# Attention beside a gated feed-forward on one core: the first head group's queries of blocks 1 to 3 spread by DMA, landing times in the plan, and four more planner figures in the table

## The chip, the cores and the metric

The kernel runs on one core of a Trainium2 chip. The metric is device time in microseconds for one execution, as a median over several runs. The profiled execution is a run of its own, with its own time; its span goes from its first to its last instruction.

## The reference

The inputs are bfloat16, with 2048 rows of 512 features. The output mixes an attention block and a feed-forward block on the same x, row by row, with a gate.

```python
g = sigmoid((x * gate_w).sum(-1, keepdims=True))
# A: attention, 32 heads of 16
q, k, v = split(x @ wqkv)                        # [32 heads, 2048, 16] each
p = softmax(q @ k.T * 16 ** -0.5)                # 2048 x 2048 per head
a = concat_heads(p @ v) @ wo
# B: feed-forward of width 1792, on x as well
b = (silu(x @ w_gate) * (x @ w_up)) @ w_down
out = g * a + (1 - g) * b
```

The greatest part of the work is the exponential: 32 heads x 2048 x 2048 values.

## The kernel before

**Tiles and units.** The 32 heads form 8 groups (G) of four. The 2048 queries form 4 blocks (QB) of 512. A group with a block is a *unit*; there are 32. The list UNIT takes group 0 of all four blocks first (units 0 to 3), and then, block by block, groups 1 to 7. Each unit has 16 (KT) *key tiles* of 128 keys, so there are 512 tiles, also called *slots* where they count time. The scores of one tile fill four PSUM banks, one for each head: 128 keys (partitions) by 512 queries.

**Two ways to the exponential.** ScalarE takes most tiles: one activation reads two or three banks and writes them to the buffer e_all (22 places of one bank). VectorE takes the others. It evicts the scores from PSUM as scaled 16-bit integers, whose bits read as bfloat16 are a rough exponential; then it makes shifted or masked copies, so that the sum of two or of four products with the values comes close to the true exponential. `groups[n]` is 2 or 4: with 2, two masked copies and a multiplication; with 4, three shifted copies, of which GpSimd makes one (`lifted`) while VectorE reads PSUM. GpSimd may also take a multiplication or a second copy (`take_over`). The integer tiles lie in tiles named c_t, or in kaug or wd_t where these have room. TensorE multiplies each copy with the values (vaug) into an output bank of the unit. These products are drained in the order of the units (`pv_list`, from the unit `closed` on). At most EB pairs of exponentials may wait in e_all before a product is forced.

**Queries.** The queries of two heads that are neighbours in a row group must not meet, so each group's queries are held twice (index v): in version v the rows of the heads with j % 2 != v are zero. For groups 1 to 7 (`q_pieces`, line 673) the queries are evicted from PSUM to the tile qst, and DMAs on the SyncE queue put each head's rows in place; VectorE and GpSimd work out a bound from them in the tile aq, whose rows follow by DMA as well. For group 0 (`q0_pieces`, line 705) the projection has padded columns; after the bound is added in PSUM, `variants` (line 733) copies the bank to qst and multiplies it on VectorE by the two columns of a mask, vsel, into the two versions. Those of blocks 0 and 1 lie in qx, those of blocks 2 and 3 in the tile on.

**The planner.** The order of all instructions on each engine is fixed while the program is built. A planner keeps a model time for each engine (`plan.pe`, `plan.dve`, `plan.act`, `plan.pool`) and a time for each PSUM bank, and takes one step after another in the loop from line 2061: scores for ScalarE, with scores of a VectorE tile alongside where `wants` asks for them (`choose`, line 877, and `emit_group`, line 985), products with values, or a piece of the other work (projections, the feed-forward, the normalising). The other work is in chains with a slot at which they are released, a deadline, and chains that they come after. A chain of queries keeps `done_at`, the slot, and `t_done`, the model time at which it was finished. `q_of[u]` is the chain that brings unit u's queries.

`v_unit` (line 2015) says from which unit VectorE may take its next tile, always the last tile that is left of that unit. Its rules, before:

```python
if y_live[0] >= NY or home_at(max(vu, au) * KT) >= 1e9 or sum(v[0] for v in vops) > 4.9 or (au, at_) < (0, 2):
    return None
while vu < UNITS:
    if vu > au + 1 or vu in q_of and not (q_of[vu].done() and (vu < QB or plan.slot >= q_of[vu].done_at + 3)):
        return None
    ...
        if plan.dve + busy + (LEAD if vu < UNITS - 1 else LAST) <= end:
            return vu
    vu += 1
```

Here `au` is the unit that ScalarE is in, `vops` are the copies and multiplications queued for VectorE, and `end` is the model time at which ScalarE would be through the tiles of the unit that are left.

**The table.** About 27 figures weigh the planner's choices: what a step is worth (W3, W4, N1, N2, NEXT ...), when side work may go (HUNGRY, KEEP, FIRST ...), limits (EB, NY), whether GpSimd takes over (TAKE_C, TAKE_P, GLEAD, WINDOW). The table WEIGHTS (line 160) holds rows of them under slot numbers, and `begin` (line 1917) puts a row in force when its slot begins.

In the profile each operation stands at the line of the helper that records it: L260 is every matmul, L263 every activation, L276 every operation of VectorE and GpSimd and every DMA of the SyncE queue in the main part.

Of the kernel before, what the change touches and what calls it, by code (L numbers as in the profile page):

```python
# [18 lines left out]
class Chain:  # L19
# [3 lines left out]
    def __init__(self, pieces, release, deadline, after=(), gap=0, cond=None, begun=()):  # L23
        self.begun = list(begun)
        self.pieces = list(pieces)
        self.i = 0
        self.owed = 0
        self.release = release
        self.deadline = deadline
        self.after = list(after)  # L30
        self.gap = gap
        self.cond = cond
        self.done_at = None
        self.t_done = 0.0

# [46 lines left out]
def kernel(  # L82
# [13 lines left out]
    P = 128  # L96
# [21 lines left out]
    EB = 10  # L118
    NE = 22
    NP = 8  # L120
    NY = 3
# [12 lines left out]
    HUNGRY = 0.351  # L134
    KEEP = 2
    FED = 5.562
    W3 = -0.276
    N1 = 6.533
    N2 = 2.473
# [15 lines left out]
    SPARE = 0.665  # L155
# [241 lines left out]
    class Plan:  # L397
        pe = dve = act = pool = 0.0
        mode = last = None
        seq = 0  # L400
        slot = -1
        chain = None

    plan = Plan()
    owed = []
    asides = []
    work_at = []
    banks = [0.0] * NP
    held = [None] * NP

    FLIP, UNIT_US, PIECE_US, COLS_US, TURN = 0.1055, 0.2157, 0.0024, 0.2133, 0.0105
    TO_ACT, ACT_FIX, ACT_COL, ACT_IN = 0.485, 0.064, 0.4265, 0.167
    ACT_PE, DVE_PE, PE_DVE, ACT_DVE = 0.055, 0.08, 0.24, 0.06
    GPS = 1
    OWN = 0
    POOL_IN, POOL_FIX, POOL_ONE, POOL_PE, POOL_OVER = 0.12, 0.12, 0.43, 0.2, 0.1
    TAKE_P = 1
    FACE = 1
    TAKE_C = 1
    GLEAD = 5.764  # L420
    WINDOW = 1.503

# [24 lines left out]
    def pay(i=0):  # L447
        ready, cost, f, c, key, fast = owed.pop(i)
        spend_v(cost, ready, key, fast)
        keep, plan.chain = plan.chain, None  # L450
        f()
        if fast:
            fast_last[0] = last_of[vec.engine.engine]
        plan.chain = keep
        if c is not None:
            c.owed -= 1
            if c.done():
                c.done_at = plan.slot
                c.t_done = plan.dve + DVE_PE
# [245 lines left out]
    def q0_pieces(qb):  # L705

        st = {}

        def landed(p):
            st["p"] = p  # L710
            later(0.6, mag, key=("aq", qb))
            later(0.21, clear, key=("aq", qb), fast=True)

        def mag():
            vec.tensor_copy(out=mt[:, 5, :], in_=st["p"][:, :])

        def clear():
            vec.tensor_scalar(out=mt[:, 5, :].bitcast(U16), in0=mt[:, 5, :].bitcast(U16), scalar1=0x7FFF, scalar2=None,
                              op0=ALU.bitwise_and)

        def bound():
            bound_add(st["p"], kneg0, mt[:, 5, :])
            spend("C", 1)
            variants(st["p"], q0[qb], work.tile([P, QBW], BF16, tag="qst", name="qst")[:, :])
        return (columns(DC, "qp", lambda dc: wpad[0][:, dc, :], lambda dc: xT[:, dc, qb * QBW:(qb + 1) * QBW], landed),
                [(1, bound, False)])

    def bound_add(p, kn, aq):
        for j in range(4):
            mm(p[32 * j:32 * j + 32, :], lhsT=kn[:, 32 * j:32 * j + 32], rhs=aq, start=False, stop=True,  # L730
               tile_position=(0, 32 * j), skip_group_check=True)

    def variants(p, to, q, more=()):

        def copy():
            vec.tensor_copy(out=q, in_=p[:, :])
            m_free(p, plan.dve)

        def select():
            for v in range(2):  # L740
                vec.tensor_scalar(out=to[:, v, :], in0=q, scalar1=vsel[:, v:v + 1], scalar2=None, op0=ALU.mult)
        key = object()
        later(0.6, copy, key=key)
        later(0.4, select, key=key, fast=True)
        for cost, f in more:
            later(cost, f, key=key)
# [238 lines left out]
    def emit_group(parts_, ds, rel):  # L985
        nonlocal quarter, at_, begun
        s = [i for p in parts_ for i in p]
        w = len(s)
        bs = next_banks(w)
        begun = 1  # L990
        start = max(plan.pe + (FLIP if plan.mode != "R" else 0.0), rel,
                    *(q_of[b // 4 // KT].t_done for b in bs if b // 4 // KT in q_of))
        spare[0] = min(spare[0] + max(0.0, horizon() - LATEST - start - 0.1), 1.5)
        plan.pe = start
        plan.mode = "R"
        for i in s:
            banks[i] = None
        for i in ds:
            banks[i] = None
        fit = fitting(w)  # L1000
        extra = len(ds) > len(fit)
        riders = (d_slots() if extra else fit)[:len(ds)]
        for k, b in enumerate(bs):
            score(psum[:, s[k], :], b, 32 if riders or w != 2 else 64)
        done = 0
        todo = []
        for p in parts_:
            e0 = e_run(len(p))
            e_next[0] = e0 + len(p)
            for k, b in enumerate(bs[done:done + len(p)]):  # L1010
                e_of[b] = e_all[:, e0 + k, :]
                e_slot[b] = e0 + k
            todo.append((p, bs[done:done + len(p)], e0))
            done += len(p)
        if riders:
            emit_d(riders, ds)
        spend("R", 2 if extra else 1)
        flush_act()
        ready = start + TO_ACT

        for p, pb, e0 in todo:
            def exp(p=p, pb=pb, e0=e0, w=len(p)):
                act(out=e_all[:, e0:e0 + w, :], in_=psum[:, p[0]:p[0] + w, :], func=ACT.Exp, scale=inv_sqrt_dh)
                plan.act = max(plan.act + ACT_FIX, ready + ACT_IN) + ACT_COL * w
                for i in p:
                    banks[i] = plan.act + ACT_PE
                for b in pb:
                    e_end[b] = plan.act + ACT_PE
            exps.append((ready, exp, len(p)))
        for _ in bs:  # L1030
            quarter += 1
            if quarter == 4:
                quarter = 0
                at_ += 1
                begun = 0
                forward()
                begun = int(quarter > 0)
            else:
                begun = 1
        begun = int(quarter > 0)  # L1040
# [193 lines left out]
    def aside_now():  # L1234
        job = asides[0]
        _, f, width, k, done, c = job
        ins = f(slice(k, k + min(width, QBW // 2)))
        if fast_last[0] is not None:
            tc.add_manual_dep(ins.ins, fast_last[0].name,
                              mybir.DependencyInfo(mybir.DependencyClass.Sync, mybir.DependencyReason.DATA), reason="beside reads of PSUM")  # L1240
        plan.pool = max(plan.pool, plan.dve + POOL_IN) + POOL_FIX + 0.48
        job[3] = k + QBW // 2
        if job[3] < width:
            return
        asides.pop(0)
        if c is not None:
            c.owed -= 1
        if done is not None:
            done()
        if c is not None and c.done():  # L1250
            c.done_at = plan.slot
            c.t_done = plan.pool + POOL_PE
# [417 lines left out]
    for g in (3, 4):  # L1670
        ones_rows(vec, g)
    for g in range(5, G):
        ones_rows(gps, g)
# [77 lines left out]
    for qb in range(1, QB):  # L1751
        d = qb * KT
        q, bd = q0_pieces(qb)
        q = pace.add(q, 0, d - 13, [known])
        bd = pace.add(bd, 0, d - 11, [q])
        need.setdefault(d - 5, []).append(bd)
        q_of[qb] = bd
    for qb in range(QB):
        for b in range(NB):
            d = UNIT.index((qb, max(2 * b, 1))) * KT  # L1760
            after = []
            if qb == 0:
                ks = []
                for tb in range(QB):
                    prev = [pace.add(k_pieces(b, tb), 3, d - 40 + tb, prev)]
                    ks += prev

                def bnd(b=b):
                    later(2.46, lambda: k_bound(b), fast=True)
                after = prev = [pace.add([(0.2, bnd, False)], 0, d - 34, ks)]  # L1770
# [3 lines left out]
            elif b == 1:  # L1774
                rel = UNIT.index((qb - 1, 6)) * KT + 1 if qb else 0
            else:
                rel = UNIT.index((qb, 2 * b - 2)) * KT + 1 if (qb, b) != (0, 2) else UNIT.index((0, 2)) * KT + 1
            q = pace.add(q_pieces(qb, b), rel, d - QLEAD, after)
            need.setdefault(d - 12, []).append(q)
            for g in {max(2 * b, 1), 2 * b + 1}:  # L1780
                q_of[UNIT.index((qb, g))] = q
# [427 lines left out]
```

## Time and profile before

| what | value |
|---|---|
| median of 3 runs | 749.18 us (749.06 to 749.56) |
| the profiled execution | 749.8 us, span 748.0 us |
| granted TensorE clock | 1.00 |
| first exponential starts | 13.26 us |
| exponentials on ScalarE | 751 instructions, 708.7 us busy |
| first evictions of VectorE's tiles | 525 instructions in c_t, kaug, wd_t |
| GpSimd busy | 276.4 us (37%) |

A share of busy time is an average over stages. Busy times of a group of instructions are unions, so that the busy time over the count is the pitch of one, which can be less than the mean duration of one where two overlap.

### The profile page before, as it was taken

To read this page: it belongs to the slowest core of one execution; us is meant where nothing else is said; L and a number is where in the kernel's file an instruction comes from. 1 tells how busy PE (TensorE), PEld (TensorE's weight loads), DVE (VectorE), ACT (ScalarE), POOL (GpSimd) and SP (SyncE) were. 2 spreads that over 40 slices of the span, in tenths; PEclk is the share of its full clock that TensorE was granted. 3 is DMA by queue.
4 is the path that set the end of the run, shared out by engine and by line. 5 is a ranking of instruction groups with operands and counts; after the bars stand their busy time and mean duration, and the time that the engine had idled before them with its cause. 6 is when DMAs were issued, how large, how long until landed. Compare 5 with 4: busy or idle time off the path is not lost.

```text
span 748.0 us, 23841 instructions
## 1 busy us (share of the span) xinstructions
PE 728.8 (97%) x10047; PEld 236.8 (32%) x10047; DVE 717.1 (96%) x1172; ACT 733.0 (98%) x823; POOL 276.4 (37%) x398
## 2 busy tenths in 40 slices
PE   8999999999999999999999999999999999999997
PEld 4323333333333333333333333333233323332332
DVE  7889999999999999999999999999999999999995
ACT  5999999999999999999999999999999999999996
POOL 5234023433454342444433423444444335343200
PEclk9999999999999999999999999999999999999999
DMA  9002012243120003221100041202001322100010
GB/s 217 18 2 58 9 33 56 59 122 87 41 56 13 13 21 92 59 55 39 36 16 22 19 104 46 66 21 59 18 13 27 76 68 58 32 20 13 15 37 30
DMA packets 91027, 34.51 MB, mean 46 GB/s; under 512 B 75488, under 2 KB 90472, under 8 KB 90920
## 3 DMA queue, kind: packets, MB, share of 16 engines
q1 hardware_dynamic: 89192, 32.66, 18.4%
q8 instruction: 79, 1.29, 0.7%
q10 hardware_dynamic: 1728, 0.33, 0.2%
q14 instruction: 28, 0.23, 0.1%
HBM read 21.55 MB, written 2.35 MB: 32 GB/s over the span
## 4 chain that ended last, share of the span: by engine, by line
ACT 60%; PE 23%; DVE 12%; issue 3%; DMA 1%; SPq 0%; DVEq 0%
ACT e_all L263 57%; PE psum L260 23%; DVE c_t L276 8%; ACT th L263 3%; DVE mt L276 1%; DVE kaug L276 1%; DVE gs L276 1%; DMA on<-osb 1%; DVE osb L276 0%; DVE kpart L276 0%; DVE qst L276 0%; SPq L276 0%; ACT xT L263 0%; DVE rd L276 0%; DVE o_t L276 0%
## 5 line engine op out<-in xcount | busy, mean ns | idle before, releaser
L263 ACT ACTIVATE e_all<-psum 128x1024 bf16<-128x1024 f32 (+1 forms) x751 | 708.7, 1113 | 1.4 <-PE psum L260 1.2
L276 DVE TENSOR_SCALAR c_t<-psum 128x512 uint16<-128x512 f32 x441 | 293.7, 689 | 8.1 <-PE psum L260 6.2
L260 PE MATMUL psum<-qx,kaug 32*128 32x512 bf16 (+1 forms) x1632 | 246.2, 385 | 7.2 <-ACT e_all L263 6.6
L276 POOL TENSOR_TENSOR c_t<-c_t,lift 128x256 int32<-128x256 int32 (+1 forms) x175 | 120.9, 700 | 177.1 <-DVE c_t L276 126.1
L260 PE MATMUL psum<-e_all,vaug 128*32 128x512 bf16 (+3 forms) x1980 | 168.2, 335 | 0.8 <-ACT e_all L263 0.4
L260 PEld LDWEIGHTS <-kaug 32*128 32x128 bf16 (+1 forms) x2048 | 74.1, 91 | 264.0 <-ACT e_all L263 188.3
L260 PEld LDWEIGHTS <-vaug 128*32 128x32 bf16 x3992 | 97.1, 95 | 130.7 <-issue 93.5
L260 PE MATMUL psum<-c_t,vaug 128*32 128x512 bf16 (+3 forms) x1720 | 134.4, 338 | 0.8 <-DVE c_t L276 0.4
L276 DVE TENSOR_SCALAR c_t<-c_t 128x2048 uint16<-128x2048 uint16 x181 | 125.4, 701 | 1.4 <-PE psum L260 0.7
L276 POOL TENSOR_TENSOR c_t<-c_t 128x256 bf16<-128x256 bf16 (+2 forms) x65 | 54.7, 858 | 98.0 <-DVE c_t L276 79.1
L260 PE MATMUL psum<-xT,wg 128*32 128x512 bf16 x896 | 73.5, 383 | 0.2 <-DVE c_t L276 0.2
L260 PE MATMUL psum<-wd_t,mt 128*32 128x512 bf16 x896 | 72.9, 382 | 0.0
L260 PE MATMUL psum<-xT,wu 128*32 128x512 bf16 x896 | 70.8, 383 | 0.9 <-DVE gs L276 0.8
L276 DVE TENSOR_SCALAR kaug<-psum 128x512 uint16<-128x512 f32 x76 | 51.1, 685 | 1.3 <-PE psum L260 0.8
L260 PE MATMUL psum<-q,kaug 32*128 32x512 bf16 (+1 forms) x256 | 49.8, 385 | 0.5 <-ACT e_all L263 0.4
L276 DVE TENSOR_TENSOR c_t<-c_t 128x2048 bf16<-128x2048 bf16 (+1 forms) x36 | 43.9, 1219 | 0.0
L260 PE MATMUL psum<-xT,wqk 128*32 128x512 bf16 x512 | 41.0, 383 | 0.2 <-DVE osb L276 0.2
L276 DVE SCALAR_TENSOR_TENSOR gs<-th,psum 128x512 bf16<-128x512 bf16 x56 | 38.1, 680 | 1.0 <-ACT th L263 0.9
L276 DVE SCALAR_TENSOR_TENSOR mt<-gs,psum 128x512 bf16<-128x512 bf16 x56 | 38.0, 679 | 0.5 <-PE psum L260 0.4
L263 ACT ACTIVATE th<-psum 128x512 bf16<-128x512 f32 x56 | 38.5, 687 | 0.0
L276 POOL TENSOR_TENSOR aq<-aq,kb 128x256 bf16<-128x256 bf16 x32 | 19.3, 612 | 40.7 <-DVE c_t L276 38.6
L260 PEld LDWEIGHTS <-mt 128*32 128x32 bf16 (+1 forms) x1045 | 24.3, 95 | 29.3 <-issue 21.3
(129 smaller groups left out, 474.0 us busy)
## 6 DMA issues: line engine op xcount, KB each, us to landing
wg<-in_B_w_gate_dram SPq DMA_DIRECT2D x56, 128.0 KB
wu<-in_B_w_up_dram SPq DMA_DIRECT2D x56, 128.0 KB
on<-osb SPq DMA_DIRECT2D x120, 16.0 KB
rb<-rr SPq DMA_DIRECT2D x15, 128.0 KB
wd_t<-in_B_w_down_dram SPq DMA_DIRECT2D x7, 256.0 KB
qx<-qst SPq DMA_DIRECT2D x96, 16.0 KB
qx<-aq SPq DMA_DIRECT2D x96, 16.0 KB
out_dram<-o_t SPq DMA_DIRECT2D x12, 128.0 KB
```

The lines of the kernel that those rows point to most:

```text
L260: return ordered(nc.tensor.matmul(out, lhsT=lhsT, rhs=rhs, **kw), [lhsT, rhs], [out])
L263: ordered(nc.scalar.activation(out=out, in_=in_, **kw), [in_, *kw.values()], [out])
L276: return ordered(f(*a, **kw), reads, [out])
```

## The change

Four things change.

1. The queries of group 0, blocks 1 to 3: the bank is still copied to qst by VectorE, but the two multiplications by the mask are gone. A new function, `apart`, issues four DMAs on the SyncE queue, each of which puts one head's 32 rows in the version where it belongs. The other version's zeros come from two GpSimd memsets at the start, put before three memsets of kaug that were there. Block 0 still uses `variants`.
2. The planner knows when queries land: each chain has a `lag`, 2.3 us for chains of queries, which is added to `t_done`. `v_unit` now asks for `t_done <= plan.pe`, in place of three slots after `done_at`; `emit_group` also waits for the queries of the unit whose VectorE tile goes alongside.
3. The projections of keys for the other groups wait until the model time of TensorE is 6.9 us (LANDED).
4. Four figures that were constants become part of each row of the table, whose rows are new but for one (slot 344): SLACK (0.04 before: how far a step may overrun a gap), LEAD (8.0 before), LINE (1.3 before: the VectorE evictions in line beyond which `wants` asks for none) and STACK (4.9 before: the queued copies and multiplications beyond which `v_unit` gives no tile). The table had 58 rows and has 52. EB in force is 7 to 10 in both.

The core of the diff, with one row of the table on each side:

```diff
-    EB = 10
+    EB = 9
...
-    HUNGRY = 0.351
+    HUNGRY = 0.08
...
-    FED = 5.562
-    W3 = -0.276
+    FED = 4.471
+    W3 = -0.428
...
-    WEIGHTS = {...
-        304: (1.015, 2, 7.758, -0.82, 0.394, 4, 0.26, 0.049, 5.632, 5.72, 1.38, 1.184, 0.96, 0.661, 8.876, 20, 3, 0.126, 9, 0, 3, 1, 1, 8.817, 1.659, 1, 0.64), ...}
+    WEIGHTS = {...
+        304: (0, 2, 7.122, 0.019, 0.063, 1.975, 0.6, 0.274, 5.198, 0, 0.699, 0.833, 1.078, 0.249, 6.964, 13, 4, 0.046, 8, 0, 4, 0, 1, 4.044, 2.0, 0, 0.653, 0.049, 5.7, 1.243, 4.62), ...}
...
+    LANDED = 6.9
...
-    GLEAD = 5.764
+    GLEAD = 5.771
+    SLACK = 0.04
+    LEAD = 7.615
+    LINE = 1.3
+    STACK = 4.9
...
     def pay(i=0):
...
-                c.t_done = plan.dve + DVE_PE
+                c.t_done = plan.dve + DVE_PE + c.lag
...
         def bound():
             bound_add(st["p"], kneg0, mt[:, 5, :])
             spend("C", 1)
-            variants(st["p"], q0[qb], work.tile([P, QBW], BF16, tag="qst", name="qst")[:, :])
+            later(0.6, lambda: apart(qb, st["p"], work.tile([P, QBW], BF16, tag="qst", name="qst")))
...
+    def apart(qb, p, q):
+        vec.tensor_copy(out=q[:, :], in_=p[:, :])
+        m_free(p, plan.dve)
+        for j in range(4):
+            r = slice(32 * j, 32 * j + 32)
+            queue.dma_start(out=q0[qb][r, j % 2, :], in_=q[r, :])

     def variants(p, to, q, more=()):

         def copy():
             vec.tensor_copy(out=q, in_=p[:, :])
             m_free(p, plan.dve)

         def select():
             for v in range(2):
                 vec.tensor_scalar(out=to[:, v, :], in0=q, scalar1=vsel[:, v:v + 1], scalar2=None, op0=ALU.mult)
...
         start = max(plan.pe + (FLIP if plan.mode != "R" else 0.0), rel,
-                    *(q_of[b // 4 // KT].t_done for b in bs if b // 4 // KT in q_of))
+                    *(q_of[u].t_done for u in {b // 4 // KT for b in bs} | ({vcur["n"] // KT if vcur else v_unit()} if ds else set()) if u in q_of))
...
     def aside_now():
...
-            c.t_done = plan.pool + POOL_PE
+            c.t_done = plan.pool + POOL_PE + c.lag
...
     for g in (3, 4):
         ones_rows(vec, g)
+    gps.memset(qx[1][:, :, 1, :], 0.0)
+    gps.memset(on_t[0][:], 0.0)
     for g in range(5, G):
         ones_rows(gps, g)
...
         bd = pace.add(bd, 0, d - 11, [q])
+        bd.lag = 2.3
         need.setdefault(d - 5, []).append(bd)
         q_of[qb] = bd
...
-                    prev = [pace.add(k_pieces(b, tb), 3, d - 40 + tb, prev)]
+                    prev = [pace.add(k_pieces(b, tb), 3, d - 40 + tb, prev, cond=lambda: plan.pe >= LANDED)]
...
             q = pace.add(q_pieces(qb, b), rel, d - QLEAD, after)
+            q.lag = 2.3
             need.setdefault(d - 12, []).append(q)
...
-    SLACK = 0.04
     CUTS = 4
-    LEAD, LAST = 8.0, 6.0
+    LAST = 6.0
...
     def v_unit():
...
-        if y_live[0] >= NY or home_at(max(vu, au) * KT) >= 1e9 or sum(v[0] for v in vops) > 4.9 or (au, at_) < (0, 2):
+        if y_live[0] >= NY or home_at(max(vu, au) * KT) >= 1e9 or sum(v[0] for v in vops) > STACK or (au, at_) < (0, 2):
             return None
         while vu < UNITS:
-            if vu > au + 1 or vu in q_of and not (q_of[vu].done() and (vu < QB or plan.slot >= q_of[vu].done_at + 3)):
+            if vu > au + 1 or vu in q_of and not (q_of[vu].done() and q_of[vu].t_done <= plan.pe):
                 return None
...
     def wants():

-        if sum(d[3] for d in d_wait) > 1.3 or not vcur and v_unit() is None:
+        if sum(d[3] for d in d_wait) > LINE or not vcur and v_unit() is None:
             return 0
         return min(2, len(d_slots()))
```

The order of a row is HUNGRY, KEEP, FED, W3, W3T, W4, W4T, W4B, N1, N2, LOW, EXTRA, NEXT, SPARE, BURST, SHORT, BACK, FIRST, EB, OWN, NY, TAKE_C, TAKE_P, GLEAD, WINDOW, FACE, LATEST, and, after the change, SLACK, LEAD, LINE, STACK.

More of the change, by code (lines that the diff above doesn't have):

```diff
@@ L34, in __init__ @@
         self.t_done = 0.0
+        self.lag = 0.0
     def left(self):
@@ L133 @@
     D_US = (0.0, 0.6, 1.133)
-    HUNGRY = 0.351
+    HUNGRY = 0.08
     KEEP = 2
-    FED = 5.562
-    W3 = -0.276
+    FED = 4.471
+    W3 = -0.428
     N1 = 6.533
-    N2 = 2.473
+    N2 = 2.494
     LOW = 1.544
@@ L1917, in begin @@
     def begin(n):
-        nonlocal HUNGRY, KEEP, FED, W3, W3T, W4, W4T, W4B, N1, N2, LOW, EXTRA, NEXT, SPARE, BURST, SHORT, BACK, FIRST, EB, OWN, NY, TAKE_C, TAKE_P, GLEAD, WINDOW, FACE, LATEST
+        nonlocal HUNGRY, KEEP, FED, W3, W3T, W4, W4T, W4B, N1, N2, LOW, EXTRA, NEXT, SPARE, BURST, SHORT, BACK, FIRST, EB, OWN, NY, TAKE_C, TAKE_P, GLEAD, WINDOW, FACE, LATEST, SLACK, LEAD, LINE, STACK
         plan.slot = n
         if n in WEIGHTS:
-            HUNGRY, KEEP, FED, W3, W3T, W4, W4T, W4B, N1, N2, LOW, EXTRA, NEXT, SPARE, BURST, SHORT, BACK, FIRST, EB, OWN, NY, TAKE_C, TAKE_P, GLEAD, WINDOW, FACE, LATEST = WEIGHTS[n]
+            HUNGRY, KEEP, FED, W3, W3T, W4, W4T, W4B, N1, N2, LOW, EXTRA, NEXT, SPARE, BURST, SHORT, BACK, FIRST, EB, OWN, NY, TAKE_C, TAKE_P, GLEAD, WINDOW, FACE, LATEST, SLACK, LEAD, LINE, STACK = WEIGHTS[n]
         for c in need.get(n, []):
```

4 lines of the change are left out of this document (2 added, 2 removed).

## The prediction

> **What bounds the kernel now.** I read the page first: shares of the span, then the chain of waits.
>
> ```profile
> span 748.0 us, 23841 instructions
> PE 728.8 (97%) x10047; PEld 236.8 (32%) x10047; DVE 717.1 (96%) x1172; ACT 733.0 (98%) x823; POOL 276.4 (37%) x398
> ACT 60%; PE 23%; DVE 12%; issue 3%; DMA 1%; SPq 0%; DVEq 0%
> ```
>
> Three engines are full together, and the chain that ended last runs mostly through ScalarE. Busy time by stretches says how much room each has between the first exponential and the tail (columns: length, then PE, PEld, DVE, ACT, POOL busy):
>
> ```profile
> 13.20:31.00 17.80, 16.98 (x219) 5.55 (x217) 14.58 (x29) 17.74 (x20) 2.38 (x4) 1.00 0.37 114
> 31.00:60.00 29.00, 28.33 (x385) 8.58 (x383) 26.66 (x50) 29.00 (x33) 10.91 (x19) 1.00 0.01 2
> 13.20:735.00 721.80, 709.28 (x9849) 227.87 (x9847) 705.15 (x1133) 720.50 (x804) 265.83 (x369) 1.00 0.18 44
> ```
>
> In these 721.8 us ScalarE idles 1.3 us, TensorE 12.5 and VectorE 16.65, of which 3.2 and 2.3 lie in the first two stretches. So ScalarE's work sets the time. It can only fall if key tiles (four heads of 128 keys by 512 queries) move from ScalarE to VectorE. The price of a tile on either side comes from the groups by operation (columns: count, then busy us and mean ns). First with shapes kept apart:
>
> ```profile
> L263 ACT ACTIVATE e_all<-psum 128x1024 bf16<-128x1024 f32 x731 | 685.0, 1102 | 1.4 <-PE psum L260 1.2
> L263 ACT ACTIVATE e_all<-psum 128x1536 bf16<-128x1536 f32 x19 | 27.8, 1541 | 0.0
> L276 DVE TENSOR_SCALAR c_t<-psum 128x512 uint16<-128x512 f32 x438 | 290.1, 685 | 7.7 <-PE psum L260 5.8
> ```
>
> Then with shapes put together, VectorE's evictions, copies and products and one of TensorE's:
>
> ```profile
> L276 DVE TENSOR_SCALAR c_t<-psum 128x512 uint16<-128x512 f32 x441 | 293.7, 689 | 8.1 <-PE psum L260 6.2
> L276 DVE TENSOR_SCALAR kaug<-psum 128x512 uint16<-128x512 f32 x76 | 51.1, 685 | 1.3 <-PE psum L260 0.8
> L276 DVE TENSOR_SCALAR wd_t<-psum 128x512 uint16<-128x512 f32 x8 | 5.3, 683 | 0.9 <-PE psum L260 0.9
> L276 DVE TENSOR_SCALAR c_t<-c_t 128x2048 uint16<-128x2048 uint16 x181 | 125.4, 701 | 1.4 <-PE psum L260 0.7
> L276 DVE TENSOR_SCALAR c_t<-kaug 128x2048 uint16<-128x2048 uint16 (+1 forms) x39 | 26.4, 692 | 0.0
> L276 DVE TENSOR_SCALAR kaug<-c_t 128x2048 uint16<-128x2048 uint16 (+1 forms) x30 | 20.7, 689 | 0.1
> L276 DVE TENSOR_SCALAR wd_t<-c_t 128x2048 uint16<-128x2048 uint16 x6 | 4.3, 717 | 0.1
> L276 DVE TENSOR_TENSOR c_t<-c_t 128x2048 bf16<-128x2048 bf16 (+1 forms) x36 | 43.9, 1219 | 0.0
> L276 DVE TENSOR_TENSOR c_t<-kaug,c_t 128x2048 bf16<-128x2048 bf16 (+1 forms) x10 | 11.8, 1179 | 0.0
> L276 DVE TENSOR_TENSOR kaug<-c_t,kaug 128x2048 bf16<-128x2048 bf16 x7 | 8.6, 1227 | 0.0
> L260 PE MATMUL psum<-c_t,vaug 128*32 128x512 bf16 (+3 forms) x1720 | 134.4, 338 | 0.8 <-DVE c_t L276 0.4
> ```
>
> The first evictions number 441 + 76 + 8 = 525, of which three take two banks: 528 banks, 132 tiles on VectorE. The exponentials take 2 x 731 + 3 x 19 and one single bank, 1520 banks, 380 tiles; together the 512 there are. A tile on ScalarE costs two double banks, 2 x 685.0/731 = 1.87 us. On VectorE it costs (350.1 evicting + 176.8 copying + 64.3 multiplying)/132 = 4.48 us, with GpSimd's share coming on top on its own engine. If VectorE gets d us free, the end comes earlier by d x 1.87/(4.48 + 1.87) = 0.295 d, since a shorter run also shortens VectorE's own time.
>
> **The change, part by part.** *Selects removed.* For query blocks 1 to 3 of head group 0 two multiplications by a mask go; the copy out of PSUM stays. (Block 0 keeps its selects.)
>
> ```profile
> 29.66 0.61 DVE L276 TENSOR_SCALAR qx<-qst,vsel 128x512 bf16<-128x512 bf16 x2
> ...
> 45.65 0.97 DVE L276 TENSOR_SCALAR on<-qst,vsel 128x512 bf16<-128x512 bf16 x2
> ...
> 79.50 0.61 DVE L276 TENSOR_SCALAR on<-qst,vsel 128x512 bf16<-128x512 bf16 x2
> ```
>
> ```profile
> 80.17 0.37 PE L260 MATMUL psum<-on,kaug 32*128 32x512 bf16 x1 [0.71 <-DVE on L276]
> 81.67 3.79 ACT L263 ACTIVATE e_all<-psum 128x1024 bf16<-128x1024 f32 x4 [0.88 <-PE psum L260]
> ```
>
> That is 0.61 + 0.97 + 0.61 = 2.19 us of VectorE, worth 0.295 x 2.19 = 0.65 us. The last two rows show a use that came at once: TensorE stood 0.71 us for the select, and ScalarE then stood 0.88 us.
>
> *DMAs added.* Each block takes four issues on SyncE, 12 in all, priced by four like ones; their landing by the nearest waits of that queue for a small transfer.
>
> ```profile
> 83.06 2.41 SPq L276 DMA_DIRECT2D q<-qst  x4
> 86.89 2.40 SPq L276 DMA_DIRECT2D q<-aq  x4
> ```
>
> ```profile
> SPq L276 <- DMA rr<-rn: 5.4, 4, 2.2
> ```
>
> ```profile
> L260 PE MATMUL psum<-q,kaug x256: 371/385/387, 103.1 to 606.0; 32*128 32x512 bf16 x93, 64*128 64x512 bf16 x35
> ```
>
> Four issues take 2.41 us, and a landing was waited for 5.4/4 = 1.35 us, at most 2.2. So a block's queries should lie ready 3.8 to 4.6 us after the copy. The planner reckons 0.08 + 2.3 = 2.38: short by 1.4 to 2.2 us. This costs nothing where the use comes later; where the planner sends a score at its earliest moment, TensorE, in order, stands with everything queued behind it. I take nothing for blocks 1 and 2 (the second had its queries at 46.6; its unit begins some ten us later) and, for block 3, that the lateness takes the place of the 0.88 us. The Trainium skill, "DMA: Bandwidth & Descriptors", section on the anatomy of one DMA (there for the GpSimd path), puts setup and completion at about 2.0 us whatever the size, and so speaks against the 2.3. With it an estimate is 2.41 + 2.0 = 4.4 us, inside the bounds above, so the trace does not contradict it, and the sum stays as it is.
>
> The four new issues can also stand ahead of the output-weight loads on SyncE, which now run early; nothing reads those weights for hundreds of us.
>
> ```profile
> 13.68 1.46 SPq L276 DMA_DIRECT2D wo_t<-in_A_wo_dram  x1
> 15.26 5.91 SPq L276 DMA_DIRECT2D wo_l<-in_A_wo_dram  x8
> ```
>
> ```profile
> L260 PE MATMUL psum<-wo_t,on x240: 379/379/391, 369.3 to 740.6; 128*32 128x512 bf16 x120
> ```
>
> *Memsets on GpSimd.* Zeros for 1024 and 2048 elements a row, put before three memsets that are there.
>
> ```profile
> L664 POOL MEMSET q<- x1: 946/946/946, 5.2 to 5.2; 128x1024 bf16 x1
> L665 POOL MEMSET qx<- x1: 1809/1809/1809, 7.3 to 7.3; 128x2048 bf16 x1
> ```
>
> ```profile
> 11.01 2.74 POOL L276 MEMSET kaug<- 128x1024 f32 x3
> 25.48 0.61 POOL L276 TENSOR_TENSOR c_t<-c_t,lift 128x256 int32<-128x256 int32 x1 [11.73 <-DVE mt L276]
> ```
>
> They cost 0.95 + 1.81 = 2.76 us, against 11.73 us in which GpSimd has nothing to do: 0. If VectorE were held for all of it, the cost would be 0.295 x 2.76 = 0.8 us; I keep that for the range.
>
> *Gates.* Keys of later head groups now wait for 6.9 us of planned time, two us later than they ran; they are due dozens of tiles later: 0. The rule "three slots after" (3 x 721.8/512 = 4.2 us) becomes "landed by plan". For a later group's queries the last issue ended at 89.3 and the first score came at 103.1, so neither form of the rule would have bound: 0.
>
> *The planner's table.* This is the greatest term and has no row of its own: every choice from the first slot on falls differently, and four more figures now vary (how long before a unit's end VectorE may still take a tile, 8.0 before, now 4.0 to 8.3; two limits on the work queued on VectorE; the slack of a gap to be filled). A shorter lead lets VectorE take tiles where it now stands at a unit's end. The gain is bounded by VectorE's 16.65 us of idle time: 0 to 4.9 us, and it may be below zero (rivals). The waits of VectorE after the start show its longest piece (columns: total us, times, longest):
>
> ```profile
> DVE c_t L276 <- PE psum L260: 6.5, 15, 1.4
> ```
>
> No piece holds a tile of 4.48 us, so only part can be gathered. I take a third, 5.5 us, which is also what the first two stretches hold: 0.295 x 5.5 = 1.6. In all 1.2 tiles more; each gives up to three more products with the values at 4 x 134.4/1720 = 0.31 us, some 1.1 us of TensorE against its 12.5 idle: hidden.
>
> Sum: 0.65 + 1.6 = 2.25 us. The profiled execution took 749.8 us, 1.8 beyond its span of 748.0, so it would come to 747.5. It lay 0.6 above the median 749.18; from the median it is 746.9, and I say 747.0.
>
> **The rivals.** *Late tiles at unit ends (slower).* In about 20 of the 32 units the lead falls to 4.0 to 5.8 us. A tile takes 4.48 us on VectorE, and a copy on GpSimd comes after that, so its last part can be ready after ScalarE's last tile of the unit. Products are drained in unit order; meanwhile ScalarE's results pile up to the limit of 7 to 10 pairs of banks. While that pile has room nothing is lost. Where it is full TensorE turns to the overdue unit, and ScalarE stands, by the only row of such a stall 0.88 us. Three such stalls eat the gain; one unit in four, 5 x 0.88 = 4.4, gives 749.18 - 2.25 + 4.4 = 751.3. For it: today's lead is 8.0, and ScalarE idles only 1.3 us. Against: the same limit on the pile is a term of the planner, which can turn to the queue in time.
>
> *Landing short (slower).* All three blocks used at once: 3 x (1.4 to 2.2) x 0.88/0.71 = 5.2 to 8.2, less the 0.88 there is and the 0.65: 752.9 to 755.9. For it: block 3's use at 80.17, 0.06 us after its selects. Against: block 2's margin. With one block it eats 0.9 to 1.8 us of the gain, no more.
>
> *Nothing to fill (no change).* The freed VectorE time stays in pieces or TensorE's 12.5 us are the next limit: the selects' 0.65 alone, 748.5.
>
> **How the numbers follow.** A measurement of this kernel can tell about 0.2%, 1.5 us, from no change. My forecast, 747.0, has a chance of 0.52; no change 0.20; late tiles 0.20; landing short 0.08. So faster 0.52, within 0.20, slower 0.28. The low end is all of VectorE's idle time used, 0.295 x (2.19 + 16.65) = 5.6: 743.6. The high end takes in late tiles with one stall more (752.2) and a part of the 0.8 for the memsets: 752.5. The forecast's own range is 743.6 to 747.6.
>
> **What would show it.** Right: fewer 128x1024 exponentials (380 tiles down to 379 or 378), VectorE idle well under 16 us between 13 and 735, ScalarE still idle about 1 to 2 us, no select on blocks 1 to 3. Wrong: ScalarE idle of several us, with TensorE standing behind DMA of queries (landing) or with waits at unit ends (late tiles); or 380 tiles or more on ScalarE, which would mean that the table bought nothing.

## The result, and the profile after

The kernel after takes 748.02 us in the median (747.63 to 748.94, 22 runs), against 749.44 us for the kernel before in the same measurement (22 runs). The ratio is 0.998, with a 95% interval of 0.9974 to 0.9987: 1.4 us faster. A second measurement on another occasion gave the same ratio, 0.998 (0.9971 to 0.9989), with 747.92 us. The profiled execution of the kernel after took 748.63 us.

From the page of the kernel after, the span, the shares and the chain of waits:

```profile
span 746.9 us, 24349 instructions
PE 734.7 (98%) x10287; PEld 242.3 (32%) x10287; DVE 715.3 (96%) x1178; ACT 732.2 (98%) x829; POOL 275.6 (37%) x391
PE 56%; ACT 33%; DVE 8%; issue 1%; DMA 1%; SPq 0%; POOL 0%; DVEq 0%; POOLq 0%
```

TensorE has 240 matmuls more, and the chain of waits that ended last now runs more through TensorE than through ScalarE. The stretches that answer to those of before (columns: length, then PE, PEld, DVE, ACT, POOL busy):

```profile
13.20:31.00 17.80, 17.06 (x220) 6.15 (x222) 13.90 (x26) 17.66 (x20) 3.27 (x4) 1.00 0.24 76
31.00:60.00 29.00, 28.68 (x371) 8.78 (x363) 26.93 (x49) 28.60 (x32) 9.68 (x16) 1.00 0.12 34
...
13.20:735.00 721.80, 716.23 (x10100) 233.48 (x10102) 702.15 (x1136) 720.78 (x811) 265.09 (x363) 1.00 0.18 44
```

In 721.8 us TensorE idles 5.6 us (12.5 before), VectorE 19.65 (16.65 before) and ScalarE 1.0 (1.3). VectorE's idle time has grown, not shrunk. The groups by operation, first the exponentials with shapes kept apart:

```profile
L264 ACT ACTIVATE e_all<-psum 128x1024 bf16<-128x1024 f32 x755 | 704.5, 1074 | 1.0 <-PE psum L261 0.8
```

and with shapes together:

```profile
L264 ACT ACTIVATE e_all<-psum 128x1024 bf16<-128x1024 f32 (+1 forms) x757 | 706.7, 1076 | 1.0 <-PE psum L261 0.8
L277 DVE TENSOR_TENSOR c_t<-c_t 128x2048 bf16<-128x2048 bf16 (+1 forms) x31 | 37.8, 1221 | 0.0
L261 PE MATMUL psum<-c_t,vaug 128*32 128x512 bf16 (+3 forms) x1904 | 147.3, 332 | 0.9 <-DVE vaug L277 0.3
```

The other two exponentials take three banks: 2 x 755 + 3 x 2 = 1516 banks, 379 tiles. So one tile has moved, 380 to 379, and the nineteen activations of three banks have nearly gone, so that there are 757 where there were 751, 2.0 us less in busy time. In the tiles c_t VectorE multiplies 31 times instead of 36 (over all tiles 46 times instead of 54), and TensorE's products with them take 147.3 us where they took 134.4. A pass is the product of one tile, or of one copy of it, with the values: four matmuls, or more where the pass is cut into parts. The whole program has 793 passes instead of 774; 414 instead of 394 belong to VectorE's tiles. With two or four parts to a tile, that is 74 tiles of four parts (and 59 of two) after, 65 (and 67) before. The new order thus spends TensorE's spare time to spare VectorE multiplications.

The first exponential starts at 13.34 us in this execution and at 12.41 in another of the same kernel (e5). So I compare from the start of the first exponential to the end of the last, which I call *the exponentials' stretch*. Its ends are in ScalarE's timeline; of the kernel before:

```profile
13.26 3.77 ACT L263 ACTIVATE e_all<-psum 128x1024 bf16<-128x1024 f32 x4 [0.16 <-PE psum L260]
...
740.60 0.84 ACT L263 ACTIVATE osb<-psum,tiny 128x256 bf16<-128x256 f32 x2 [0.52 <-PE psum L260]
```

and of the kernel after:

```profile
13.34 2.86 ACT L264 ACTIVATE e_all<-psum 128x1024 bf16<-128x1024 f32 x3 [0.16 <-PE psum L261]
...
739.54 0.84 ACT L264 ACTIVATE osb<-psum,tiny 128x256 bf16<-128x256 f32 x2 [0.62 <-PE psum L261]
```

740.60 - 0.52 - 13.26 = 726.82 us before, 739.54 - 0.62 - 13.34 = 725.58 after: 1.24 less. The second execution of the kernel after (e5), which starts its first exponential at 12.41, gives 725.55, so this measure repeats to some hundredths. Of the kernel before there is one profiled execution. The ends in e5, and in e6 below:

```profile
738.58 0.84 ACT L264 ACTIVATE osb<-psum,tiny 128x256 bf16<-128x256 f32 x2 [0.62 <-PE psum L261]
...
739.72 0.84 ACT L264 ACTIVATE osb<-psum,tiny 128x256 bf16<-128x256 f32 x2 [0.62 <-PE psum L261]
```

### The profile page after: what moved, and what is told of

Its sections match the earlier page's. It is cut to its first block, busy times and chain, and to the rows that moved or that the text cites. A ratio compares the mean times of both kernels' runs of the same rounds, so it can differ in the third digit from the quotient of the medians.

```text
span 746.9 us, 24349 instructions
## 1 busy us (share of the span) xinstructions
PE 734.7 (98%) x10287; PEld 242.3 (32%) x10287; DVE 715.3 (96%) x1178; ACT 732.2 (98%) x829; POOL 275.6 (37%) x391
## 4 chain that ended last, share of the span: by engine, by line
PE 56%; ACT 33%; DVE 8%; issue 1%; DMA 1%; SPq 0%; POOL 0%; DVEq 0%; POOLq 0%
PE psum L261 56%; ACT e_all L264 31%; DVE c_t L277 5%; ACT th L264 2%; DMA wu<-in_B_w_up_dram 1%; DVE kaug L277 1%; DVE mt L277 0%; DMA on<-osb 0%; DVE gs L277 0%; DVE osb L277 0%; DVE on L277 0%; SPq L277 0%; DVE wd_t L277 0%; DVE kpart L277 0%; POOL c_t L277 0%
## 5 line engine op out<-in xcount | busy, mean ns | idle before, releaser
L264 ACT ACTIVATE e_all<-psum 128x1024 bf16<-128x1024 f32 (+1 forms) x757 | 706.7, 1076 | 1.0 <-PE psum L261 0.8
L277 DVE TENSOR_SCALAR c_t<-psum 128x512 uint16<-128x512 f32 (+1 forms) x430 | 286.0, 687 | 9.1 <-PE psum L261 7.0
L277 POOL TENSOR_TENSOR c_t<-c_t,lift 128x256 int32<-128x256 int32 (+1 forms) x159 | 114.5, 729 | 174.1 <-DVE c_t L277 143.9
L261 PE MATMUL psum<-c_t,vaug 128*32 128x512 bf16 (+3 forms) x1904 | 147.3, 332 | 0.9 <-DVE vaug L277 0.3
L261 PEld LDWEIGHTS <-vaug 128*32 128x32 bf16 x4232 | 101.8, 95 | 130.4 <-issue 88.4
L277 DVE TENSOR_SCALAR c_t<-c_t 128x2048 uint16<-128x2048 uint16 (+2 forms) x190 | 129.7, 689 | 1.2
L277 POOL TENSOR_TENSOR c_t<-c_t 128x256 bf16<-128x256 bf16 (+3 forms) x60 | 53.7, 906 | 89.0 <-DVE c_t L277 64.2
L277 DVE TENSOR_SCALAR kaug<-psum 128x512 uint16<-128x512 f32 x84 | 55.8, 684 | 0.5 <-PE psum L261 0.2
L261 PE MATMUL psum<-q,kaug 32*128 32x512 bf16 (+1 forms) x256 | 46.9, 385 | 0.1
L277 DVE TENSOR_TENSOR c_t<-c_t 128x2048 bf16<-128x2048 bf16 (+1 forms) x31 | 37.8, 1221 | 0.0
L277 POOL TENSOR_TENSOR c_t<-kaug,lift 128x256 int32<-128x256 int32 (+1 forms) x32 | 21.9, 691 | 36.3 <-DVE c_t L277 23.7
```

The costliest lines, as they stand in the source:

```text
L261: return ordered(nc.tensor.matmul(out, lhsT=lhsT, rhs=rhs, **kw), [lhsT, rhs], [out])
L264: ordered(nc.scalar.activation(out=out, in_=in_, **kw), [in_, *kw.values()], [out])
L277: return ordered(f(*a, **kw), reads, [out])
```

## The experiments

Theory A, from the prediction: the number of tiles on ScalarE sets the time, and VectorE's freed time is worth something only where it takes a tile. Its rivals are named with each run. Two kinds of edit have to be kept apart. An edit that the plan does not see keeps the order of every instruction that is left; an edit that the plan sees draws a new order. I call such a new order a *draw*.

**e1: the order of before, DMAs in place of the selects.** The plan still reckons with the selects.

```diff
         def select():
-            for v in range(2):
-                vec.tensor_scalar(out=to[:, v, :], in0=q, scalar1=vsel[:, v:v + 1], scalar2=None, op0=ALU.mult)
+            if to is q0[0]:
+                ...  # block 0 as before
+                return
+            for j in range(4):
+                r = slice(32 * j, 32 * j + 32)
+                queue.dma_start(out=to[r, j % 2, :], in_=q[r, :])
...
+    gps.memset(qx[1][:, :, 1, :], 0.0)
+    gps.memset(on_t[0][:], 0.0)
```

> The order of the kernel before is kept to the instruction; only the six multiplications by the mask become twelve DMAs, and the two memsets come in. 380 tiles stay on ScalarE. Theory A (the time follows the number of tiles, freed VectorE time that takes no tile is worth nothing, and a landing shows where the use comes at once): blocks 1 and 2 cost nothing; at block 3 TensorE's wait behind the queries grows from 0.71 us to 3.2 to 4.0 us (landing 3.8 to 4.6 us after the copy ends at 79.47), ScalarE's stall there grows from 0.88 to 3 to 4.5 us: 2 to 4 us slower than before. Theory B (the selects themselves were on the path): 0.65 to 2.2 us faster than before, with no wait on the DMA over 1 us.

Measured: 752.77 us, 3.1 slower than before (749.66 in the same measurement); ratio 1.0048 (1.0035 to 1.0061). The waits of TensorE name the cause (columns: total us, times, longest):

```profile
PE psum L260 <- DMA on<-qst: 2.5, 1, 2.5
PE psum L260 <- DMA qx<-qst: 1.4, 1, 1.4
```

and the timeline shows block 3:

```profile
79.93 0.68 DVE L276 CAST qst<-psum 128x512 bf16<-128x512 f32 x1
...
80.63 2.41 SPq L276 DMA_DIRECT2D on<-qst  x4
83.06 0.37 PE L260 MATMUL psum<-on,kaug 32*128 32x512 bf16 x1 [2.46 <-DMA on<-qst]
...
84.55 3.78 ACT L263 ACTIVATE e_all<-psum 128x1024 bf16<-128x1024 f32 x4 [2.62 <-PE psum L260]
```

The copy ends at 80.61. The score, which reads the rows of one head, runs at 83.06: 2.45 us from the end of the copy to the first use, not the 3.8 to 4.6 expected for a whole block. By the semaphore that it waits for, it needs the second of the four issues, which starts at 81.19; the signals of the four come 1.78 to 1.87 us after the start of each issue, the last at 84.32, 3.7 us after the copy. So the whole block took about as long as the low end of what was expected, but the first use did not need the whole block. ScalarE's stall there is 2.62 us, below the 3 to 4.5 expected. Block 1, for which nothing was expected, stood 1.4 us. By the starts of the exponentials e1 falls behind the kernel before by 1.3 us at block 1 and by 1.7 more at block 3. So the total falls within the 2 to 4 of theory A in part by luck: only 1.7 of the 3.1 us arise where it put them. Theory B (faster) is out for this order as a whole; whether some gain from the freed VectorE time hides under the two waits, e1 does not show.

**e2 and e6: the order of after, selects in place of the DMAs.** e6 repeats e2 on one chip with e5, the unchanged kernel after.

```diff
     def apart(qb, p, q):
         vec.tensor_copy(out=q[:, :], in_=p[:, :])
         m_free(p, plan.dve)
-        for j in range(4):
-            r = slice(32 * j, 32 * j + 32)
-            queue.dma_start(out=q0[qb][r, j % 2, :], in_=q[r, :])
+        for v in range(2):
+            vec.tensor_scalar(out=q0[qb][:, v, :], in0=q[:, :], scalar1=vsel[:, v:v + 1], scalar2=None, op0=ALU.mult)
```

> The order of the kernel after is kept; its twelve DMAs of group 0's queries become six multiplications on VectorE again, 2.2 us of VectorE time that the plan doesn't know. 379 tiles stay on ScalarE. Theory A: no more than 0.3 us from the kernel after, so about 748.1, and about 1.3 us faster than before. Theory B: 0.65 to 2.2 us slower than the kernel after, 748.7 to 750.2, so that the gain is gone.

> The kernel after, unchanged, on one chip with the next run. 0.998 of before, as measured.

> The order of the kernel after with the six multiplications in place of the twelve DMAs, now on one chip with the kernel after. Theory A (only the tiles count): within 0.3 us of the kernel after. Theory B (2.2 us more on VectorE reach the end in part, even where no tile moves): 0.6 to 1.3 us slower than the kernel after, as the traces of the first pair had it (725.6 against 726.6 us from the first exponential to the last).

Measured: e2 748.91 us (ratio to before 0.9992, 0.9984 to 1.0001); e5 747.92 and e6 748.90 (ratio to before 0.9992, 0.9983 to 1.0). So the six selects cost 1.0 us with no tile moved: theory A's 0.3 is wrong and theory B right. (This is their price in an order that was planned without them. What they cost in an order with room planned for them, as in the kernel before, is not shown.) The stretches agree: 726.59 (e2) and 726.56 (e6) against 725.55 (e5). Where the first part of the 1.0 us arises shows at block 1. In e6 VectorE's timeline has the selects between two steps that follow each other at once in e5:

```profile
29.21 0.68 DVE L277 CAST qst<-psum 128x512 bf16<-128x512 f32 x1
30.00 0.62 DVE L277 TENSOR_SCALAR qx<-qst,vsel 128x512 bf16<-128x512 bf16 x2
30.54 0.18 DVE L277 COPY rb<-gw_col 128x4 bf16<-128x4 bf16 x1
```

ScalarE's timeline of e5:

```profile
12.41 17.52 ACT L264 ACTIVATE e_all<-psum 128x1024 bf16<-128x1024 f32 x19 [0.17 <-PE psum L261]
29.76 0.68 ACT L264 ACTIVATE mt<-mt 128x512 bf16<-128x512 f32 x1
30.29 22.16 ACT L264 ACTIVATE e_all<-psum 128x1024 bf16<-128x1024 f32 x24
```

and of e6:

```profile
12.54 17.52 ACT L264 ACTIVATE e_all<-psum 128x1024 bf16<-128x1024 f32 x19 [0.17 <-PE psum L261]
29.89 0.68 ACT L264 ACTIVATE mt<-mt 128x512 bf16<-128x512 f32 x1
30.41 22.74 ACT L264 ACTIVATE e_all<-psum 128x1024 bf16<-128x1024 f32 x24
```

The same 24 exponentials take 22.16 us without the selects and 22.74 with them, 0.58 more, and not one wait is shown. Of the 0.58, 0.43 lie inside busy time (22.16 against 22.59 us): an exponential starts later and overlaps its predecessor less. The other 0.15 are three pauses of less than 0.1 us each, too short for the view of waits. Counted from each run's first exponential, the starts in e6 lie 0.58 us behind those of e5 after block 1, still 0.58 after block 2 and 1.03 after block 3; from there on the lag stays between 1.02 and 1.04 to the end, so this fixed order did not catch up. Over all exponentials, 0.7 of the 1.0 us are busy time and 0.3 idle time; the group is 706.7 busy and 1.0 idle in e5, and in e6:

```profile
L264 ACT ACTIVATE e_all<-psum 128x1024 bf16<-128x1024 f32 (+1 forms) x757 | 707.4, 1070 | 1.3 <-PE psum L261 0.8
```

**e3 and e4: less TensorE, both orders kept.**

```diff
         for i, b in enumerate(range(4 * n, 4 * n + 4)):
+            if k == 3 and not first and not last:
+                break
             j = HEADS[i]
```

> Leaves out, in the order of the kernel before, the product with the values of the fourth copy of each four-part tile, 65 passes of 774 (about 20 us of TensorE at 0.31 us each). Every exponential, eviction and copy stays. If ScalarE alone sets the end (theory A): within 1 us of before. If TensorE sets it in places: up to 6 us faster.

> The same in the order of the kernel after: 69 passes of 793 left out, about 21 us of TensorE. TensorE idles 5.6 us there between 13.2 and 735 us, against 12.5 before. Theory A: within 1 us of the kernel after (748). Rival (the new table has made TensorE the second bound): 2 to 6 us faster than the kernel after, and a greater gain than the same cut brings to the kernel before.

Measured: e3 748.63 us, ratio to before 0.9988 (0.9979 to 0.9996), 1.0 us; e4 747.11, ratio to before 0.9969 (0.9957 to 0.9981), which is 0.9 us under the 748.0 of the kernel after. By the exponentials' stretch it is 0.5 us in e3 (726.29) and 1.0 in e4 (724.60). The products in c_t and the stretch from 13.2 to 735 us, e3 first, then e4 (which leaves out 69 of the 74 fourth products, since five of them begin or end the sum of a unit):

```profile
L260 PE MATMUL psum<-c_t,vaug 128*32 128x512 bf16 (+3 forms) x1416 | 115.9, 340 | 0.7 <-DVE c_t L276 0.4
13.20:735.00 721.80, 704.19 (x9517) 222.85 (x9509) 704.54 (x1132) 720.57 (x805) 265.40 (x368) 1.00 0.18 44
...
L261 PE MATMUL psum<-c_t,vaug 128*32 128x512 bf16 (+3 forms) x1596 | 125.9, 330 | 1.2 <-DVE c_t L277 0.4
13.20:735.00 721.80, 711.02 (x9776) 229.22 (x9772) 702.64 (x1139) 720.99 (x813) 264.53 (x363) 1.00 0.18 44
```

The products fall by 18.5 us in e3 and 21.4 in e4, TensorE's busy time as a whole only by 5.1 and 5.2; where the rest went, these runs do not show. The cut is worth 0.5 to 1 us in either order. So TensorE is not what sets the time, although the chain of the kernel after names it for 56%; the rival's 2 to 6 us are out.

**e7 and e9: code and table, each alone.** e7 is the code of after with the rows of before (the four new figures at 0.04, 8.0, 1.3 and 4.9); e9 is the code of before with the rows of after.

> The code of the kernel after (DMAs, lags, gates, the wait of the keys), with the table and the first figures of the kernel before; SLACK, LEAD, LINE and STACK at their old constants. The plan that comes out has 386 tiles on ScalarE, against 380 before and 379 after. Theory A (time follows the tiles at 1.8 us each): 10 to 12 us slower than before, about 760. Rival (the code of the change is itself worth the 0.65 us of the selects or more, and the table only adds to it): 0 to 2 us faster than before.

> The table of the kernel after with its 31 figures, and all else of the code as before: selects on VectorE, three slots as the gate, no lag, no wait of the keys, no memsets. 384 tiles on ScalarE. Theory A (each tile more on ScalarE costs 2.3 to 2.6 us, as the two other draws showed): 9 to 11 us slower than before. Rival (the table is better in itself): faster than before, or no more than 2 us slower.

**e8 and e10: a new draw from an edit without meaning.** The kernels before and after with one figure of the model moved.

```diff
-    MUL_US = 1.135
+    MUL_US = 1.14
```

> The kernel before with one figure of the model moved that is no part of the change: MUL_US, the time that the plan gives a multiplication, 1.140 in place of 1.135. No operation changes in kind. The plan falls otherwise and has 385 tiles on ScalarE. Theory A: 8 to 10 us slower than before: a table fits one order alone, and any edit that the plan sees loses more than the whole change gains. Rival (the planner is robust to 0.4% in one figure): within 1.5 us of before.

> The kernel after with MUL_US 1.140 in place of 1.135, which is no part of the change. 382 tiles on ScalarE, three more than after. Theory A: 7 to 8 us slower than the kernel after, about 755. Rival (the new table is the more robust one): within 2 us of it.

**e11: the four figures held.** SLACK, LEAD, LINE and STACK at 0.04, 8.0, 1.3 and 4.9 in all rows of after.

> The kernel after with SLACK, LEAD, LINE and STACK at their old constants in every row; the other 27 figures of the rows as they are. 384 tiles on ScalarE, five more than after. Theory A: 11 to 13 us slower than the kernel after, 759 to 761, which is no more per tile than an edit that means nothing costs. Rival (the shorter lead costs time at unit ends): faster than the kernel after or within 1 us of it, with fewer waits of ScalarE.

What the five draws gave (busy time and waits of the exponentials from the groups and the waits of ScalarE):

| run | tiles on ScalarE | exponentials busy | their waits | stretch | median us |
|---|---|---|---|---|---|
| before | 380 | 708.7 | 1.2 | 726.8 | 749.44 |
| after | 379 | 706.7 | 0.8 | 725.6 | 748.02 |
| e7 code alone | 386 | 720.9 | 2.9 | 740.6 | 763.45 |
| e9 table alone | 384 | 717.2 | 5.6 | 740.6 | 763.51 |
| e8 before, MUL_US | 385 | 717.6 | 4.6 | 740.3 | 762.53 |
| e10 after, MUL_US | 382 | 713.5 | 13.0 | 745.0 | 768.71 |
| e11 four figures held | 384 | 716.1 | 2.8 | 737.7 | 759.98 |

Against before, e7 is 1.0188 (1.0172 to 1.0203), e9 1.0188 (1.0171 to 1.0205), e8 1.0173 (1.0159 to 1.0187), e10 1.0259 (1.0244 to 1.0274) and e11 1.0144 (1.0129 to 1.0159). The direction of theory A held in all five. Its size held for e11 alone; e7, e8 and e9 cost 2 to 3.4 us more than it allowed, and e10 13 more. The tiles are not the whole price: the exponentials' waits come on top. In e10 they are the greater part:

```profile
ACT e_all L264 <- PE psum L261: 13.0, 8, 5.5
```

with, in its timeline, the longest one:

```profile
467.47 4.69 ACT L264 ACTIVATE e_all<-psum 128x1024 bf16<-128x1024 f32 x5 [5.54 <-PE psum L261]
```

Busy time plus waits explains the draws to about 2 us: stretch less both is 16.8 to 18.8 in all seven rows (the other activations, where they do not overlap the exponentials).

These runs do not show what the code or the four figures are worth each. One figure moved by 0.4% costs 13 us and 21 us. The code alone costs 14, the table alone 14, the four figures held 12: no more than an edit that means nothing. Only edits that keep the order (e1 to e6) tell the parts apart. What a table searched anew for the code with the four figures held would give was not tried, and stays open. One part of the change is without effect: without the lag of the later head groups' queries, the same program comes out, instruction for instruction.

## Why the prediction was right, and where it was not

The forecast was 2.25 us faster by the sum, and 747.0; 1.4 to 1.6 were measured. The direction, the whole range (743.6 to 752.5) and the mark of 379 tiles held. The forecast's own range, 743.6 to 747.6, was missed by 0.4, and another mark failed: VectorE's idle time rose where it was to be well under 16 us. That the sum came as near as it did is partly luck: its two terms erred in opposite directions, one too small and one too large. The parts:

- *Selects, 0.65.* Measured 1.0 (e6 against e5), in an order that has no room planned for them. The route was wrong: 0.295 per us supposed that VectorE's freed time must be turned into tiles. In the fixed order some 2.2 us of VectorE came to the end as 1.0, about 0.45 per us, without a tile moving. The step that failed is the reading of ScalarE's idle time, 1.3 us, as all that late scores cost: of the 1.0 us, 0.7 lay inside the exponentials' busy time, 0.43 of it in 24 activations behind block 1.
- *Table, 1.6.* Mis-sized. With the selects in place in both orders, 726.82 (before) against 726.56 (e6) leaves 0.3 us for the new order, 0.6 to 0.75 by the medians, whose interval reaches no change (0.9983 to 1.0). The mechanism was another: no idle time of VectorE was gathered (16.65 to 19.65). One tile moved while nine more tiles got four parts. Over all its tiles VectorE multiplies 9.4 us less, copies 7.1 more and evicts 2.5 more: the trade by itself pays for the tile, to 0.2 us, and the time of the selects went into VectorE's idle time. That fits the lines, but no run changes the parts alone. And the tile brought less than 1.87 us: with the selects in both, the exponentials' busy time fell from 708.7 to 707.4 (e6), 1.3. Pairs of banks took the place of seventeen activations of three banks, six instructions more in all. In the trace of before, the next exponential starts 1.335 us after one of three banks and 0.921 after a pair, so the 51 banks take some 0.8 us more in pairs, about the missing 0.6.
- *TensorE's cover.* The 1.1 us of added products were 19 passes, 5.9 us at 0.31 each; TensorE's idle time fell by 6.9 of its 12.5. It still covered most of them: leaving out 69 passes brings 1.0 us in the new order and 0.5 in the old (e4, e3).
- *Landing, short by 1.4 to 2.2.* The size for a whole block was about right (3.7 us, against 3.8 to 4.6), but it was the wrong thing to wait for. The sum took four issues and a landing; the score needs one head's rows, in e1 2.45 us after the copy against the plan's 2.38. The mechanism is real: with the old order, planned for selects, it costs 3 us (e1). In the kernel after TensorE shows no wait on a DMA of queries; the 0.71 us wait of before is gone; the closest use, in block 1, comes 0.13 us after its rows have landed (33.40 and 33.27). The Trainium skill's 2.0 us ("DMA: Bandwidth & Descriptors", anatomy of one DMA, there for the GpSimd path) is near what e1 shows at block 3: 1.8 us from the start of an issue on SyncE to its signal. The prediction added it to the whole time of four issues; from the start of the last, 1.8 us after that of the first, the estimate would be 3.8.
- *Memsets and gates, 0.* Right as far as seen: the lag of the later groups' queries changes no instruction, and GpSimd idles 18 us between its last memset and its first lift, by its timeline in the kernel after:

```profile
15.51 0.96 POOL L277 MEMSET kaug<- 128x1024 f32 x1
34.64 0.61 POOL L277 TENSOR_TENSOR c_t<-c_t,lift 128x256 int32<-128x256 int32 x1 [18.17 <-DVE c_t L277]
```

- *Late tiles at unit ends.* Not seen as waits: those of the exponentials are 0.8 us in all. Lateness inside busy time would not show there. e11 cannot speak for or against the shorter lead.
- *Nothing to fill.* This rival had part of the truth: VectorE's freed time stayed in pieces, and its 748.5 lies nearer the measured 748.02 than the 747.0 does. But the time fell by more than its 0.65 us, and one tile did move.
- *The price of a tile on VectorE, 4.48.* It left out two small groups in wd_t, copies of 2.1 us and a multiplication of 1.2; with them it is 4.50, which changes nothing.

## What to carry to other kernels

Where a program's order is drawn by a planner, first keep the order fixed and change the operation alone: six selects against twelve DMAs read cleanly at 1.0 us in one order and at 3 us the other way in another. A new draw lost 11 to 21 us here whatever the edit meant, so a part of a change is not judged by taking it out and letting the plan run again. The same twelve DMAs gained 1.0 us in the order planned with their landing time and lost 3 us in the order planned without it; that the landing time in the plan is what made the difference was not tested alone.

## What the runs showed of the hardware that I had not expected

ScalarE's busy time can hold lateness that the view of waits does not name. In the last long run of exponentials of the kernel after, those of two banks follow each other at 66.31/72 = 0.921 us, though each lasts 1.07 us in the mean, so one begins before the last has ended:

```profile
672.62 66.31 ACT L264 ACTIVATE e_all<-psum 128x1024 bf16<-128x1024 f32 x72
```

The mean of all 755 there is 704.5/755 = 0.933, and in e6 it was 22.74/24 = 0.948 behind the selects, with no wait shown. From start to start the difference is plainer: the closest starts among those 24 lie 0.903 us apart in both runs, in e5 none comes more than 1.00 us after the one before, and in e6 three come 1.08 to 1.22 after it. An engine near 100% by the busy column can thus still be fed late. The pitch, against the best pitch of the same instruction in the same trace, tells.
